# Infini-attention with a gated feed-forward on one core: another written-out order of the operations, the memory summed before it is masked, tanh in place, six probability buffers

## The chip, the cores and the metric

The kernel runs on one core of a Trainium2 chip. The metric is the device time of one execution in microseconds (us), the median of several runs. The core has TensorE (PE in the profile), VectorE (DVE), ScalarE (ACT), GpSimd (POOL) and SyncE (SP, which here only issues transfers). Each has its own queue of instructions and works through it in order: an instruction that waits holds all those behind it.

## The reference

```python
xn = layernorm(x)                       # x: 1 x 2048 x 448
q, k, v = xn @ wq, xn @ wk, xn @ wv     # 16 heads of 28, 4 segments of 512 rows
for s in range(4):                      # M = 0, z = 0 before the first segment
    p = softmax(causal(qs @ ks.T * 28**-0.5))      # inside the segment
    a_dot = p @ vs
    pq = phi(qs)                                   # phi(t) = t + 1 if t > 0 else exp(t)
    a_mem = (pq @ M) / (pq @ z + 1e-6)             # M, z from the earlier segments
    o = sigmoid(beta) * a_mem + (1 - sigmoid(beta)) * a_dot
    M = M + phi(ks).T @ vs;  z = z + sum(phi(ks))
s = concat(o) @ wo
f = (gelu(xn @ w_gate) * (xn @ w_up)) @ w_down     # inner width 1792
out = x + s * silu(f)
```

## The kernel before

A segment of 512 rows is four blocks of 128. Every piece of work is an operation with a name: the first digit after the letters is the segment, the next the block, step or chunk. Those that matter below:

- Start: `x00`, `x01`, `x02` load the blocks of the first segment (`x02` two of them, from ScalarE's queue; the other two from SP's), `warm_up` (L433) is eight matmuls on a zeroed tile, `bn`, `ag`, `xn`, `xc` are the layer norm (L489, L491, L514, L524), `trc` transposes (L457), `wv0`, `wk0`, `wq0` with a block's digit are projections (L575; seven matmuls to a block: the two half-width ones of two blocks are issued side by side as a "visit", `wr`). `nrm` with `rq` is part of a test of the logits' size: a column maximum and one small matmul.
- Attention of a segment: ten score steps `sc` (L846; sixteen 32-row matmuls with K = 32, into two pairs of PSUM banks), two exps to a step, `ex` (L861, ScalarE, 128 x 1024), causal masks `mk` on POOL (L872), products with the values `pv` (L908, sixteen matmuls a block). PSUM has four banks in two pairs, `pp0` and `pp1`, and four single ones, `ps0` to `ps3`. In segments 0 and 1 a score step may also write into `ps0` and `ps1`.
- Memory: `up` (L721) multiplies phi(k) with v of a finished segment; the matrix has all pairs of four heads, and `bdmask` keeps the blocks of a head with itself. `um` (L733), `ma` (L736) and `mc` (L739) make the masked bf16 memory `mbd` of it; `rd` (L759) reads it with phi(q). phi is an exp on ScalarE (`ex` of wq or wk, L687), a minimum on POOL (`mi`, L692), and `ph` on VectorE (L700 for q, L705 for k). The sums go out to DRAM and come back as reciprocals over the partitions (`den`, `dc`, `dg`, `rc`, `rd`, `rb`); `sm` (L770), `ca` (L814) and `cb` (L817) join both parts.
- Feed-forward: `gu` (gate and up, L964 for segment 0, L998 for the others), `ge` (gelu, L1005), `hm` (product, L1010, into `hT`), `dn` (down projection, L1055, fourteen matmuls a block), `th` and `sg` (L1064, L1067: tanh and a product; with it silu), `wo` (L1085), `fm`, `fa`, `st` (product, sum with x, store).

The feed-forward of a segment stands between the attention of two: gate and up of segment s, then the attention of segment s together with its down projections and the q, k, v of the next one. The table `TURNS` names all operations in one order. `arrange` (L157) walks it with assumed durations, gives every buffer the slot that comes free first, and returns the operations by the starts it has worked out; instructions are issued in this order, so it sets the order in all queues. Waits on the chip come from the data and buffers alone.

The lines of the memory, `s` being the segment that ended:

```python
um:  um[:] = u * bdmask                (VectorE, from PSUM)
ma:  macc[:] = macc[:] + um[:]         (POOL)
mc:  mbd[:] = macc[:]                  (POOL, cast to bf16)
```

Of the kernel before, what the change touches and what calls it, by code (L numbers as in the profile page):

```python
# [89 lines left out]
x00 x02 va0 warm qs1 va1 warm_up x01 wv vb1 ez0 qs2 ones wv2 kn0 qs4 nhalf wv3 wk vb0 kn1 bd wk2 ident wk3  # L90
bn00 ez1 xc_z su2 ag00 wq xc0 ep00 wq2 su3 trc00 xc2 bn01 bd0 evc00:ACT trc02 red_z qs0 wq3 xc3 evc02:ACT wv00
ag01 wgh xc1 sv2 trc03 qs3 wuh pw00 trc01 sv3 wv02 evc03:DVE evc01:DVE wv03 table wg0 xn00 ep03 wv01 ep01 wu0
ep02 pw02 wg4 wr0 pw03 wk00 evwv00:ACT du00 xn02 wu4 wk01 evwv02:ACT du02 xn03 x1 tr00 evwv03:DVE bd1 wk03
pw01 sq0 wg8 ev00:DVE wk02 sq1 xn01 du03 sq2 du01 wr1 evwv01:DVE wo0 wq03 evwk02:DVE evwk01:ACT wq01 sq3
evwk03:DVE evwk00:ACT tr01 rq2 tr02 tr03 sq4 ev01:DVE tk00 wq02 ev03:DVE exwk01 wq00 ev02:DVE rq1 exwk00 gh00
tk02 rq0 sq5 rq3 miwk00 gu00 evwq02:ACT wu8 rq5 evwq00:ACT miwk01 rq4 gu01 evwq01:ACT tq00 evwq03:DVE bn13
gu02 bn10 tq02 ge00 bn12 ge01 ag10 hm00 gu03 sq6 tq03 hm01 sq7 bn11 gh02 tk01 ag12 ag13 ag11 ep10 rq7 pw10
gu04 ge03 tq01 xn10 ge02 hm03 gu05 xn13 ge04 du10 du13 rq6 tr10 hm04 gu06 ge05 hm02 tr13 hm05 nrm gu07 nrm2
wo_in0 x2 xn11 gh06 xn12 x3 phwk00 wd_in0 gu08 ge07 tk03 du11 du12 hm07 gu09 ge08 tr11 ge06 hm08 gu010 hm06
ge09 wo_in3 tr12 bn20 gu011 hm09 bn21 wd_in1 bn23 beta gh010 bn30 ag30 gu012 ag20 ge011 bn22 ge010 bn33 hm011  # L100
gu013 ge012 hm010 hm012 sc00 ge013 ag21 ag23 ag22 wq10 ep20 hm013 pw20 wq11 bn31 wr1wq0 ex000 ag31 evwq10 ag33
ex001 bn32 tq10 sc01 wv10 xn20 ex010 xn22 xn21 gx mk000c0 ag32 evwq11 ex011 sc02 xn23 du20 dn000 ex020 mk011c0
tr20 phwk01 ex021 sc03 dn005 tr23 mk001c0 ex030 mk010c384 mk021c256 dn0010 mk020c0 ex031 tq11 bd2 mk011c384
wv11 mk010c0 th00 sc04 mk020c256 tr21 wr1wv0 sg00 mk021c0 ex040 bd3 evwv11 pv02 ex041 evwv10 tr22 mk040c0 sc05
mk031c0 ou000 wk10 ex050 ep30 mk040c384 wk11 wo_in1 pw30 ex051 sc06 mk041c0 wr1wk0 mk030c0 ex060 evwk10
mk041c384 wq12 mk050c0 evwk11 tk10 wq13 ex061 mk060c0 mk051c0 pv04 exwk10 mk061c384 tk11 wr1wq2 ou010
mk060c384 sc07 gates wk13 miwk10 evwq12 ex070 dn010 evwq13 tq12 mk061c0 ex071 xn30 gates2 sc08 dn015 ex080
den000 mk071c256 mk070c256 den010 xn31 dn0110 ex081 xn32 tq13 xn33 sc09 du30 phwk10 wk12 ex090 tr30 wr1wk2
th01 up0 mk081c0 evwk12 mk080c0 ex091 sg01 mk071c0 tk12 wv12 mk070c0 evwk13 exwq10 wv13 mk091c384 macc mk091c0
wr1wv2 tk13 mk090c384 exwq11 sc10 evwv13 mk090c0 pv07 miwq10 pv09 tr32 ou020 ex100 dn020 miwq11 ou030 ex101  # L110
evwv12 den020 wv20 phwq10 den030 wv21 tr33 sc11 wr2wv0 ex110 wv23 evwv21 dn025 dc00 evwv20 ex111 phwq11 tr31
dn0210 sc12 th02 mk100c0 wv22 dg00 ex120 rc00 mk111c384 wr2wv2 mc0 sg02 rd003 wq32 ex121 mk101c0 evwv23 wq33
rd000 mk110c0 evwv22 mk120c0 exwk11 rd11 rd002 mk121c0 sc13 ou111 mk110c384 wr3wq2 rd001 ex130 wq21 mk120c256
evwq33 xw10 mk111c0 rd10 evwq32 ex131 mk121c256 wq20 xw11 miwk11 ou101 rd12 den111 wr2wq0 ou121 sc14 rb000
wk20 evwq21 ex140 rb010 wk21 phwk11 wo_in2 ex141 wr2wk0 rb030 pv12 mk140c384 evwk21 mk141c384 sc15 evwq20
mk141c0 wq22 ex150 evwk20 tq20 wq23 cb00 ex151 dn030 tk20 mk140c0 wr2wq2 sc16 mk150c0 evwq23 dn035 mk131c0
# [40 lines left out]
def arrange(ops):  # L157
# [7 lines left out]
    for turn in order:  # L165
# [14 lines left out]
        if e == "POOL" or e == "DVE" and o.alone:  # L180
            s = max(s, port["DVE" if e == "POOL" else "POOL"])
# [5 lines left out]
        if e == "POOL" or e == "DVE" and o.alone:  # L187
            port[e] = s + occ
# [1423 lines left out]
```

## Time and profile before

| | us |
|---|---|
| median of three runs (229.08, 228.65, 228.87) | 228.87 |
| the profiled execution, whole | 230.46 |
| its span in the trace | 228.7 |
| around the span (230.46 - 228.7) | 1.76 |
| PE busy in the span | 218.6 |
| ACT, DVE, POOL busy | 158.5, 151.3, 125.9 |

The profiled execution took 1.59 us more than the median. Durations below are of that execution. A row of the timeline gives start, duration, engine, line, operation, output and inputs, the number of instructions in a row, and in brackets the idle time ahead of the first with what ended it. In rows by stretches every engine's busy time stands with its count, then the clock that TensorE was granted (1.00 is full), the share of the transfer engines and the rate of transfer. "Chain" rows are the chain of work that ended last, in order of time.

### The profile page before, as it was taken

How to read it: one execution, taken by the hardware profiler on the slowest of the kernel's cores; microseconds unless marked ns; L12 is line 12 of the kernel's file. 1: busy time of each engine (PE TensorE's matmuls, PEld its weight loads, DVE VectorE, ACT ScalarE, POOL GpSimd, SP SyncE). 2: the span in 40 equal slices, each digit the busy share in tenths (PEclk: the TensorE clock that was granted, in tenths of full speed). 3: DMA queues.
4: the chain of work that ended last, by engine and by line, in shares of the span. 5: the costliest groups of instructions: out<-in, count | busy, mean ns of one | idle time of the engine just before them, and what ended most of it. 6: DMA issues, size and time to landing. Idle time of an engine off the chain costs nothing.

```text
span 228.7 us, 4944 instructions
## 1 busy us (share of the span) xinstructions
PE 218.6 (96%) x1819; PEld 99.1 (43%) x1822; DVE 151.3 (66%) x285; ACT 158.5 (69%) x215; POOL 125.9 (55%) x223
## 2 busy tenths in 40 slices
PE   7999999899999999999999999999989999999990
PEld 3544343244443444444444344455533444445560
DVE  4699879936888867557756484677836457449152
ACT  4798335989978775999488779955777976335120
POOL 7422100569557598953076984270699975364620
PEclk9999999889999999999999999999999999999999
DMA  6899789493335799312655034125170111744012
GB/s 221 208 342 219 162 243 264 119 200 68 75 74 70 197 184 161 78 47 66 195 156 139 4 79 92 27 65 153 57 198 21 34 44 26 195 122 121 23 42 52
DMA packets 45606, 27.69 MB, mean 121 GB/s; under 512 B 30936, under 2 KB 40984, under 8 KB 45576
## 3 DMA queue, kind: packets, MB, share of 16 engines
q1 hardware_dynamic: 44600, 26.60, 49.6%
q10 hardware_dynamic: 976, 0.71, 1.0%
q8 instruction: 16, 0.26, 0.5%
q14 instruction: 14, 0.11, 0.2%
HBM read 17.38 MB, written 2.98 MB: 89 GB/s over the span
## 4 chain that ended last, share of the span: by engine, by line
PE 74%; DVE 15%; DMA 3%; issue 2%; POOL 2%; ACT 1%; ACTq 1%; SPq 1%; DVEq 0%; POOLq 0%
PE ps L1055 15%; PE ps L998 14%; PE pp L998 14%; PE ps L575 10%; PE pp L846 5%; PE ps L1085 5%; PE ps L908 4%; DVE hT L1010 3%; DVE st L489 2%; DMA x_sb<-in_A_x_dram 2%; DVE um L1151 2%; PE ps L721 1%; PE ps L759 1%; PE pp L1055 1%; PE ps L1121 1%
## 5 line engine op out<-in xcount | busy, mean ns | idle before, releaser
L861 ACT ACTIVATE pt<-pp 128x1024 bf16<-128x1024 f32 x76 | 73.9, 1028 | 16.3 <-PE pp L846 16.2
L872 POOL TENSOR_SCALAR_AFFINE_SELECT pt<-pt 128x256 bf16<-128x256 bf16 x128 | 50.5, 425 | 18.7 <-ACT pt L861 18.5
L1055 PE MATMUL ps<-wd_sb,hT 128*128 128x448 bf16 x196 | 43.0, 362 | 0.2 <-DVE e L611 0.2
L1005 ACT ACTIVATE gl<-pp 128x512 bf16<-128x512 f32 x29 | 17.0, 596 | 20.7 <-PE pp L998 12.2
L998 PEld LDWEIGHTS <-wg_sb 64*128 64x128 bf16 x252 | 22.8, 94 | 15.2 <-issue 2.5
L998 PEld LDWEIGHTS <-wu_sb 64*128 64x128 bf16 x252 | 23.1, 94 | 14.3 <-issue 0.4
L1055 PEld LDWEIGHTS <-hT 128*128 128x128 bf16 x210 | 19.5, 99 | 20.6 <-issue 5.3
L1005 ACT ACTIVATE gl<-ps 128x512 bf16<-128x512 f32 x27 | 15.6, 596 | 12.4 <-PE ps L998 9.7
L575 PEld LDWEIGHTS <-xnT 128*128 128x128 bf16 (+1 forms) x192 | 14.6, 97 | 20.4 <-issue 11.0
L1010 DVE TENSOR_TENSOR hT<-gl,ps 128x512 bf16<-128x512 bf16 x27 | 18.3, 682 | 7.6 <-ACT gl L1005 7.4
L817 POOL TENSOR_TENSOR oT<-oa,om 128x512 bf16<-128x512 f32 x12 | 15.7, 1317 | 12.4 <-DVE oa L814 12.4
L1010 DVE TENSOR_TENSOR hT<-gl,pp 128x512 bf16<-128x512 bf16 x29 | 19.1, 675 | 5.1 <-ACT gl L1005 5.1
L770 POOL TENSOR_TENSOR om<-om,rb 128x512 f32<-128x512 f32 x12 | 15.1, 1266 | 13.3 <-DMA rb<-rdr 11.8
L1076 POOL TENSOR_TENSOR oo<-sg,x_sb 128x448 bf16<-128x448 f32 (+1 forms) x14 | 14.6, 1049 | 12.2 <-DVE sg L1093 3.2
L692 POOL TENSOR_SCALAR e<-e 128x896 bf16<-128x896 bf16 (+1 forms) x12 | 11.8, 986 | 13.5 <-ACT e L687 13.4
L507 POOL TENSOR_TENSOR rs<-rs,nhalf 128x1 f32<-128x1 f32 (+1 forms) x7 | 5.3, 758 | 24.6 <-DVE rs L502 20.9
L998 PE MATMUL ps<-xnT,wu_sb 64*128 64x512 bf16 x63 | 17.0, 377 | 0.5 <-DVE hT L1010 0.5
L998 PE MATMUL ps<-xnT,wg_sb 64*128 64x512 bf16 x63 | 17.2, 377 | 0.0
L998 PE MATMUL pp<-xnT,wg_sb 64*128 64x512 bf16 x63 | 17.0, 376 | 0.0
L998 PE MATMUL pp<-xnT,wu_sb 64*128 64x512 bf16 x63 | 17.0, 376 | 0.0
L998 PE MATMUL pp<-xn,wg_sb 64*128 64x512 bf16 x63 | 17.0, 376 | 0.0
L998 PE MATMUL ps<-xn,wu_sb 64*128 64x512 bf16 x63 | 17.0, 376 | 0.0
(137 smaller groups left out, 425.9 us busy)
## 6 DMA issues: line engine op xcount, KB each, us to landing
rb<-rdr SPq DMA_DIRECT2D x28, 256.0 KB
out_dram<-oo SPq DMA_DIRECT2D x15, 112.0 KB
wd_sb<-in_B_w_down_dram SPq DMA_DIRECT2D x2, 784.0 KB
x_sb<-in_A_x_dram SPq DMA_DIRECT2D x3, 448.0 KB
xn<-xnT SPq DMA_DIRECT2D x6, 192.0 KB
rdr<-dc SPq DMA_DIRECT2D x28, 32.0 KB
wg_sb<-in_B_w_gate_dram SPq DMA_DIRECT2D x2, 384.0 KB
wu_sb<-in_B_w_up_dram SPq DMA_DIRECT2D x2, 384.0 KB
```

Source lines behind the costliest of these rows:

```text
L575: nc.tensor.matmul(out=self.bank.ap()[:, 0:D], lhsT=self.xT.ap()[r, c, n * P:(n + 1) * P], rhs=self.w[r, c, :], **kw)
L692: o = gps(f"mi{nm}{s}{half}", n / 1024, lambda: nc.gpsimd.tensor_scalar(out=t(), in0=t(), scalar1=1.0, scalar2=0.0, op0=ALU.min, op1=ALU.max),
L770: oU[s, g, 1] = t, gps(f"sm{s}{g}", 1.22, lambda t=t, r=r: nc.gpsimd.tensor_tensor(out=t.ap(), in0=t.ap(), in1=r.ap(), op=ALU.mult), deps= ...
L817: oT[s][1].append(gps(f"cb{s}{g}", 1.22, lambda g=g, t=t, tm=tm: nc.gpsimd.tensor_tensor(out=dst.ap()[:, g, :], in0=t.ap(), in1=tm.ap(), o ...
L846: nc.tensor.matmul(out=S2[i // 2].ap(i % 2)[:, c0:c0 + n], lhsT=kT[s][0].ap()[r, g, kb * P:(kb + 1) * P], rhs=qT[s][0].ap()[r, g, kb * P:L ...
L861: nc.scalar.activation(out=dst, in_=src, func=ACT.Exp, scale=scale)
L872: nc.gpsimd.affine_select(out=v, in_=v, pattern=[[0, 2], [1, P]], compare_op=ALU.is_ge, fill=0.0, base=0, channel_multiplier=-1)
L998: nc.tensor.matmul(out=bf[fc].ap(i), lhsT=w, rhs=x, start=c == 0, stop=c == 2 * NC3)
L1005: a = act(f"ge{s}{fc}", L, lambda: nc.scalar.activation(out=gl.ap(), in_=bf[fc].ap(0), func=ACT.Gelu_apprx_tanh), func="gelu", deps=[o], a ...
L1010: nc.vector.tensor_tensor(out=hT[s][0].ap()[:, fc, :], in0=gl.ap(), in1=bf[fc].ap(1), op=ALU.mult), deps=[a] + held,
L1055: nc.tensor.matmul(out=bank.ap()[:, 0:D], lhsT=hT[s][0].ap()[:, fc, b * P:(b + 1) * P], rhs=wd_sb[:, fc, :], start=(fc == 0), stop=(fc == ...
L1076: o = op(f"fa{s}{b}{h}", eng, lambda: (nc.vector if o.on == "DVE" else nc.gpsimd).tensor_tensor(out=oo.ap()[:, r], in0=t.ap()[:, r], in1=x ...
```

## The change

1. `TURNS` is another table; it reorders all five queues.
2. `arrange` returns the operations in the table's own order, and its rule for VectorE and POOL working at once, and some assumed durations, are others. That has an effect through order and slots only.
3. Memory: `macc` is added up unmasked, on VectorE straight from PSUM; the mask is applied in the cast on POOL. The tile `um` and two `ma` are gone.
4. `th` writes into the tile of `sg`, and the pool of two tanh tiles is gone.
5. Six buffers for the probabilities in place of five.
6. Loads and the first load of ScalarE's table no longer stand in a fixed sequence; the first exps of segment 0 no longer have to stand behind its last gelu.

```diff
 TURNS = """
-x00 x02 va0 warm qs1 va1 warm_up x01 wv vb1 ez0 qs2 ones wv2 kn0 qs4 nhalf wv3 wk vb0 kn1 bd wk2 ident wk3
-bn00 ez1 xc_z su2 ag00 wq xc0 ep00 wq2 su3 trc00 xc2 bn01 bd0 evc00:ACT trc02 red_z qs0 wq3 xc3 evc02:ACT wv00
+va0 qs0 kn1 vb0 nhalf warm warm_up x01 kn0 x00 x02 wv3 wv table wv2 qs2 xc_z bn01 su2 bn00 ag00 ez1 ident x1
+wk2 wk wk3 wq2 wuh wq wu0 va1 wgh bd bd0 qs4 qs1 vb1 qs3 xc0 trc00 su3 ep00 ag01 xc1 xc2 xc3 trc01 ep01 pw00
...
-    return sorted(ops, key=lambda o: o.start)
+    return [named[turn.partition(":")[0]] for turn in order]
...
-        um = const.tile([P, G, P], F32, name="um")
+        red_t = const.tile([P, P], F32, name="red")
...
-        pt_p = slots(5, [P, HG, L], BF16, "pt")
+        pt_p = slots(6, [P, HG, L], BF16, "pt")
...
-        th_p = slots(2, [P, D], F32, "th")
...
         def load(eng, name, dst, src, kb, rate=320.0):
-            o = op(name, {eng: (0.5, 2.0)}, ..., after=first[-1:], prio=-1000, kb=kb, rate=rate)
+            o = op(name, {eng: (0.5, 1.5)}, ..., prio=-1000, kb=kb, rate=rate)
...
         table_op = op("table", ..., func=ACT.Exp),
-            deps=[nhalf_in], after=wv_in, prio=-400)
+            deps=[nhalf_in], prio=-400)
...
             if s == 0:
-                o = dve("macc", ..., lambda: nc.vector.tensor_tensor(
-                    out=macc[:], in0=uv(), in1=bd, op=ALU.mult), deps=[o] + bd_in, ...)
+                o = dve("macc", ..., lambda: nc.vector.tensor_copy(out=macc[:], in_=uv()), deps=[o], ...)
             else:
                 o = dve(f"um{s}", ..., lambda: nc.vector.tensor_tensor(
-                    out=um[:], in0=uv(), in1=bd, op=ALU.mult), deps=[o, mem["acc"], ok_op], ...)
-                o = gps(f"ma{s}", 1.22, lambda: nc.gpsimd.tensor_tensor(
-                    out=macc[:], in0=macc[:], in1=um[:], op=ALU.add), deps=[o], prio=pr)
-            mem["acc"] = o
-            mem["cast"] = gps(f"mc{s}", 0.58, lambda: nc.gpsimd.tensor_copy(out=mbd[:], in_=macc[:]), ...)
+                    out=macc[:], in0=macc[:], in1=uv(), op=ALU.add), deps=[o, mem["cast"]], ...)
+            mem["cast"] = gps(f"mc{s}", 1.22, lambda: nc.gpsimd.tensor_tensor(
+                out=mbd[:], in0=macc[:], in1=bd, op=ALU.mult), deps=[o] + bd_in, ...)
...
-                            after=[first] if exps else [first, att.get("gelu_end")],
+                            after=[first, att.get("gelu_end") if s and not exps else None],
...
             a = act(f"th{s}{b}", D, lambda: nc.scalar.activation(
-                out=th.ap(), in_=bank.ap()[:, 0:D], func=ACT.Tanh, scale=0.5), ...)
+                out=t.ap(), in_=bank.ap()[:, 0:D], func=ACT.Tanh, scale=0.5), ...)
             ... vector.scalar_tensor_tensor(
-                out=t.ap(), in0=th.ap(), scalar=1.0, in1=bank.ap()[:, 0:D], ...)
+                out=t.ap(), in0=t.ap(), scalar=1.0, in1=bank.ap()[:, 0:D], ...)
```

A few lines of the changed kernel have other numbers: L491 is L493, L542 is L544, L611 is L613, L692 is L694, L700 is L702, L705 is L707, L721 is L723, and the cast of the memory is L738.

The first place is VectorE at the start of segment 0's attention. `hT` is the product of the feed-forward, `st`, `mv`, `rs` and `xn` belong to the layer norms of segments 2 and 3, `qs`, `kn`, `e` and `vaug` receive the projections of segment 1 out of PSUM, and L705 is phi(k) of segment 0. Before:

```order
L1010 TENSOR_TENSOR hT_85<-gl0_127,ps3_95 128x512
L489 BN_STATS st0_138<-x_sb3_66 128x6
L491 BN_AGGR mv0_142<-st0_138 128x2
L611 CAST qs_107<-ps1_93 128x16x28
L491 BN_AGGR mv0_142<-st3_141 128x2
L489 BN_STATS st2_140<-x_sb3_66 128x6
L514 TENSOR_SCALAR xn0_96<-x_sb2_65,mv1_143,rs0_144 128x448 x3
L491 BN_AGGR mv0_142<-st2_140 128x2
L611 CAST e1_106<-ps2_94 128x16x28
L514 TENSOR_SCALAR xn0_96<-x_sb2_65,mv1_143,rs0_144 128x448
L542 COPY xn0_96<-xn0_96 128x4x64
L705 SCALAR_TENSOR_TENSOR kn0_86<-kn0_86,e0_105 128x32x28
```

After, at the same place:

```order
L1010 TENSOR_TENSOR hT_85<-gl2_130,ps2_94 128x512
L493 BN_AGGR mv1_142<-st0_137 128x2
L707 SCALAR_TENSOR_TENSOR kn0_86<-kn0_86,e0_105 128x32x28
L613 CAST qs_107<-ps3_95 128x16x28
L1151 TENSOR_REDUCE red_83<-pt1_109 64x16
L613 CAST kn1_87<-ps2_94 128x16x28
L445 TENSOR_SCALAR igate_79<-igate_79 128x2
L613 CAST e0_105<-ps0_92 128x16x28
L613 CAST kn1_87<-ps1_93 128x16x28
L613 CAST vaug1_89<-ps2_94 128x16x28
L613 CAST vaug1_89<-ps3_95 128x16x28
L707 SCALAR_TENSOR_TENSOR kn0_86<-kn0_86,e1_106 128x32x28
```

The layer norm of segment 2 has moved ahead, into the feed-forward, that of segment 3 behind; six evictions stand together, and a phi(k), a reduction and a gate (L445) stand ahead of some of them. On PE, step `sc01` writes `pp0` and `pp1` now, where before it wrote `ps0`, `ps1` and `pp0`.

The second place is VectorE in the gate and up of segment 1. L700 is phi(q) of segment 2 (`pqT`), the L1010 rows are `hm`, which read the banks that later `gu` steps write. Before:

```order
L705 SCALAR_TENSOR_TENSOR kn0_86<-kn0_86,e1_106 128x32x28
L744 COPY oa3_116<-ps2_94 128x512
L744 COPY oa2_115<-ps3_95 128x512
L1010 TENSOR_TENSOR hT_85<-gl2_129,pp1_91 128x512
L1010 TENSOR_TENSOR hT_85<-gl0_127,pp0_90 128x512
L700 SCALAR_TENSOR_TENSOR pqT0_104<-qT0_100,e1_106 128x1024
L1010 TENSOR_TENSOR hT_85<-gl1_128,ps1_93 128x512
L1010 TENSOR_TENSOR hT_85<-gl2_129,ps3_95 128x512
```

After:

```order
L707 SCALAR_TENSOR_TENSOR kn0_86<-kn0_86,e1_106 128x32x28
L1010 TENSOR_TENSOR hT_85<-gl2_130,pp1_91 128x512
L744 COPY oa3_117<-ps3_95 128x512
L744 COPY oa2_116<-ps2_94 128x512
L1010 TENSOR_TENSOR hT_85<-gl0_128,ps1_93 128x512
L1010 TENSOR_TENSOR hT_85<-gl1_129,pp0_90 128x512
L1010 TENSOR_TENSOR hT_85<-gl0_128,ps3_95 128x512
L702 SCALAR_TENSOR_TENSOR pqT0_104<-qT0_100,e1_106 128x1024
```

phi(q) has moved behind two more products.

The third place is POOL around the second memory update, at the change from segment 2's feed-forward to segment 3's attention. Before:

```order
L770 TENSOR_TENSOR om3_120<-om3_120,rb3_124 128x512
L1076 TENSOR_TENSOR oo0_136<-sg1_133,x_sb1_64 128x448
L817 TENSOR_TENSOR oT0_126<-oa0_113,om3_120 128x512
L736 TENSOR_TENSOR macc_81<-macc_81,um_83 128x512
L739 CAST mbd_82<-macc_81 128x512
L817 TENSOR_TENSOR oT0_126<-oa2_115,om1_118 128x512
L872 AFFINE_SELECT pt3_111<-pt3_111 128x2x128 x2
```

After:

```order
L770 TENSOR_TENSOR om2_120<-om2_120,rb3_125 128x512
L770 TENSOR_TENSOR om0_118<-om0_118,rb0_122 128x512
L1076 TENSOR_TENSOR oo1_136<-sg3_134,x_sb1_64 128x448
L738 TENSOR_TENSOR mbd_82<-macc_81,bdmask_80 128x512
L1076 TENSOR_TENSOR oo0_135<-sg1_132,x_sb1_64 128x448
L770 TENSOR_TENSOR om1_119<-om1_119,rb2_124 128x512
L817 TENSOR_TENSOR oT0_127<-oa0_114,om1_119 128x512
L872 AFFINE_SELECT pt4_112<-pt4_112 128x2x128
```

One row writes the memory `mbd` where two did, and it stands inside the feed-forward of segment 2. On PE the matmuls of that update (`up2`) stand behind step `sc26` of segment 2's attention, before behind `sc30`.

More of the change, by code (lines that the diff above doesn't have):

```diff
@@ L100 @@
[L100 to L104, printed above, removed]
@@ L187, in arrange @@
         if e == "POOL" or e == "DVE" and o.alone:
-            port[e] = s + occ
+            other = port["DVE" if e == "POOL" else "POOL"]
+            if other[0] <= s < other[1]:
+                s = other[1]
+            port[e] = s, s + occ
         if o.kb is not None:
@@ L350, in load @@
         def load(eng, name, dst, src, kb, rate=320.0):
-            o = op(name, {eng: (0.5, 2.0)}, lambda: (nc.sync if eng == "SP" else nc.scalar).dma_start(
-                out=dst, in_=src), after=first[-1:], prio=-1000, kb=kb, rate=rate)
+            o = op(name, {eng: (0.5, 1.5)}, lambda: (nc.sync if eng == "SP" else nc.scalar).dma_start(
+                out=dst, in_=src), prio=-1000, kb=kb, rate=rate)
             first.append(o)
@@ L1043, in down @@
         def down(s, b, pr):
[L1044 removed]
+            bank, t = Buf(B_, END if s == LAST else ONE), Buf(sg_p)
             o = None
```

168 lines of the change are left out of this document (86 added, 82 removed).

## The prediction

> **What bounds the kernel now.** I read the busy times first, then the chain of work that ended last, then stretches, then the waits of TensorE.
>
> ```profile
> PE 218.6 (96%) x1819; PEld 99.1 (43%) x1822; DVE 151.3 (66%) x285; ACT 158.5 (69%) x215; POOL 125.9 (55%) x223
> ...
> PE 74%; DVE 15%; DMA 3%; issue 2%; POOL 2%; ACT 1%; ACTq 1%; SPq 1%; DVEq 0%; POOLq 0%
> ```
>
> TensorE is busy for 96% of the span and carries 74% of the chain. The change leaves its matmuls as they are, so it can gain only where TensorE stands idle or runs slowly, and it loses where it makes new such places. The stretches say where these are:
>
> ```profile
> core 0: us, PE busy (x) PEld busy (x) DVE busy (x) ACT busy (x) POOL busy (x), PEclk, DMA share, GB/s
> 6.10:38.60 32.50, 32.23 (x185) 14.06 (x189) 28.54 (x75) 19.99 (x38) 6.19 (x8) 1.00 1.01 237
> 38.60:50.70 12.10, 10.88 (x79) 4.03 (x79) 8.28 (x23) 10.98 (x15) 5.86 (x13) 0.86 0.79 176
> 103.80:106.00 2.20, 1.65 (x17) 0.69 (x15) 2.17 (x6) 2.17 (x3) 0.50 (x1) 1.00 0.39 119
> 167.00:169.00 2.00, 1.12 (x7) 0.41 (x5) 0.30 (x1) 1.67 (x3) 1.94 (x4) 1.00 0.84 227
> ...
> 223.10:228.70 5.60, 0.18 (x5) 0.03 (x1) 1.25 (x4) 0.25 (x1) 0.32 (x1) 0.97 0.21 53
> ```
>
> ```profile
> PE ps L759 <- POOL mbd L739: 0.9, 1, 0.9
> PE ps L846 <- DVE qs L611: 0.7, 1, 0.7
> PE ps L998 <- DVE hT L1010: 0.5, 1, 0.5
> ```
>
> The worst is 38.6 to 50.7, the start of segment 0's attention, with 1.2 us idle and a clock of 0.86. Small holes stand at 104 and 168. The last 5.6 us after TensorE's last matmuls (a silu, products, sums and a store) have the same steps after the change, and I cost them at nothing. Inside the worst stretch:
>
> ```profile
> 40.60:44.00 3.40, 2.28 (x22) 0.84 (x21) 3.37 (x11) 3.40 (x5) 0.86 (x2) 1.00 0.35 83
> 44.00:47.50 3.50, 3.50 (x13) 1.16 (x12) 1.56 (x3) 3.21 (x6) 3.14 (x7) 0.51 0.78 177
> ...
> 38.56:59.44 20.88, 19.62 (x153) 7.71 (x153) 14.94 (x37) 19.76 (x28) 13.17 (x29) 0.92 0.60 134
> ```
>
> TensorE is busy for 67% (2.28 of 3.40) of one stretch, and in the next, about as long, it runs at half the clock. Over the 20.88 us between the steps sc00 and sc09 the clock of 0.92 means 0.08 x 20.88 = 1.67 us lost, and ScalarE is busy for 19.76 of the 20.88: it is the true bound there.
>
> **The change part by part.** *Segment 0's attention.* Full rates, from the chain in order of time:
>
> ```profile
> 54.47 0.66 PE ps L908 x16
> 55.13 0.29 PE ps L575 x2
> ...
> 55.75 0.67 PE ps L575 x3
> 56.42 0.95 PE ps L1055 x5
> 59.51 0.33 PE pp L846 x8
> ```
>
> That is 0.66 us for a value product, 0.145 for a half-width matmul, 0.19 for a matmul of 448 columns, 0.33 for a score step. Before, sc00 to sc09 holds 9 steps (2.97), 27 projection matmuls (5.13), 8 half-width ones (1.16), 28 of the down projection (5.32) and two value products (1.32): 15.9 us in 20.88, so 5.0 lost, 1.67 of it by the clock. After, the order puts about 19.1 us of the same kind there (three more projections, five blocks' worth of half-width matmuls, dn020, up0): work that was later is drawn into the holes. What holds ScalarE:
>
> ```profile
> 38.95 1.28 ACT L861 ACT_TABLE_LOAD   x1
> 40.24 1.94 ACT L861 ACTIVATE pt<-pp 128x1024 bf16<-128x1024 f32 x2
> 46.35 1.94 ACT L861 ACTIVATE pt<-pp 128x1024 bf16<-128x1024 f32 x2 [0.29 <-PE pp L846]
> 48.74 0.54 ACT L1064 ACTIVATE th<-ps 128x448 f32<-128x448 f32 x1 [0.45 <-PE ps L1055]
> 55.12 1.01 ACT L687 ACTIVATE e<-kn 128x896 bf16<-128x896 bf16 x1
> ```
>
> The table is loaded 1.67 us after sc00 starts; 18 exps at 0.97 are 17.5, one exp of phi 1.0, one tanh 0.54: 20.7 us at least. So the loss is at least 20.7 - 19.1 = 1.6, and at most 3.4 could be gained. VectorE's queue there:
>
> ```profile
> 44.31 1.29 DVE L705 SCALAR_TENSOR_TENSOR kn<-kn,e 128x896 bf16<-128x896 bf16 x1
> ```
>
> Before, sc01 waits 0.7 for a cast (the second row of the list of waits), which stands behind layer norms. After, these are gone, but the phi(k) of 1.29 in this row stands ahead of the casts. So I take a loss of 2.2 to 2.4 rather than 1.6, a gain of 2.6 against the profiled execution. Against the median I take less. This execution is 1.59 us above the median, almost the 1.67 that the half clock costs, which would fit if the timed runs did not have it. Without it the loss before is 3.3, and the gain 1.0. I take -1.0, with ends -3.4 and +3.0 (below).
>
> *Feed-forward of segment 1, step gu18.*
>
> ```profile
> 101.73 1.04 POOL L692 TENSOR_SCALAR e<-e 128x1024 bf16<-128x1024 bf16 x1
> 102.81 1.23 DVE L700 SCALAR_TENSOR_TENSOR pqT<-qT,e 128x1024 bf16<-128x1024 bf16 x1 [2.45 <-POOL e L692]
> 103.76 0.38 PE L998 MATMUL ps<-xnT,wg_sb 64*128 64x512 bf16 x1
> 104.69 0.37 PE L998 MATMUL ps<-xnT,wu_sb 64*128 64x512 bf16 x1 [0.55 <-DVE hT L1010]
> ```
>
> phi(q) stands idle for 2.45 us at the head of VectorE's queue, waiting for POOL; the product behind it is late, and its bank with it. The two matmuls of a pair lie side by side, so rows follow each other at about half of 0.38; from 103.76 to 104.69 TensorE loses 0.7. After, two more products stand ahead of phi(q), and that bank is free in time: -0.7, ends -0.7 and 0. What is late next is the product behind hm16, whose bank is wanted several steps later.
>
> *The second memory update.*
>
> ```profile
> 166.96 1.26 POOL L736 TENSOR_TENSOR macc<-macc,um 128x512 f32<-128x512 f32 x1
> 168.29 0.61 POOL L739 CAST mbd<-macc 128x512 bf16<-128x512 f32 x1
> ...
> 166.19 1.88 PE L1055 MATMUL ps<-wd_sb,hT 128*128 128x448 bf16 x9
> ...
> 171.71 2.98 POOL L872 TENSOR_SCALAR_AFFINE_SELECT pt<-pt 128x256 bf16<-128x256 bf16 x8 [0.51 <-ACT pt L861]
> ```
>
> TensorE's first read of the memory waits for the cast (0.9 in the list of waits). Nine matmuls at 0.19 from 166.19 end at 167.9, the read starts 0.9 after the modelled end of 168.07, so 1.05 us are lost. After, the update stands a whole feed-forward earlier, and its one POOL instruction inside that feed-forward: -1.05. POOL's price of an update falls from 1.26 + 0.61 = 1.87 to one tensor operation, which I take at 1.26 (bf16 out of f32, two inputs; ends 0.61 and 1.87). On VectorE the sum has the same shape as the masked product, no change. But POOL's sums of both parts now move into segment 3's attention: eight tensor operations (10.1) and twelve masks at 0.37 (4.5) are 14.6 us behind sc30 before pv32 can start, which TensorE reaches after about 15 us of its own work. I add +0.4, ends 0 and +1.4. Together -0.65.
>
> *Start.*
>
> ```profile
> 1.26 3.60 PE L433 MATMUL ps<-oT 128*128 128x512 bf16 x8 [1.26 <-DVE oT L386]
> 4.65 0.63 PE L457 MATMUL ps<-oT,hT 128*128 128x128 bf16 x4
> 6.09 0.93 PE L575 MATMUL ps<-wv_sb,xnT 128*128 128x448 bf16 x3
> ...
> 2.79 0.63 DVE L489 BATCH_NORM_STATS2 st<-x_sb 128x6 f32<-128x448 bf16 x1 [1.59 <-DMA x_sb<-in_A_x_dram]
> ```
>
> Block 0 is loaded first on SP's queue before, and its statistics start at 2.79. After, the layer norm of block 0 needs the second transfer of that queue, and all four groups of transposes stand ahead of the first projection. One transfer later I put at about 0.9 us for the transposes and 0.8 for the projections, of which later order takes back a part: +0.5, ends 0 and +1.0. The logit test's matmul leaves the stretch 6.1 to 38.6, which has 0.27 us idle: -0.25, ends -0.27 and 0.
>
> *Around the last values.*
>
> ```profile
> 210.24 4.01 POOL L817 TENSOR_TENSOR oT<-oa,om 128x512 bf16<-128x512 f32 x3 [0.72 <-DVE oa L814]
> ...
> 215.87 0.92 PE L1085 MATMUL ps<-wo_sb,oT 128*128 128x448 bf16 x4
> ```
>
> POOL is done at 214.25, wo at 215.87 reads the result: 1.6 us in hand. After, the last two value products (pv37, pv39) stand behind steps gu32 and gu33, some 3 us later, and the rest of that chain with them. 3 - 1.6 = +1.4 is the upper end, 0 the lower; I take +0.3, since down projections can run meanwhile.
>
> *Small ones.* TensorE's changes between tile shapes fall by two of 132; three projection matmuls at 0.19 are 0.57, and take 0.67 in the row at 55.75 behind a score step, so a change costs 0.1: -0.2, ends -0.2 and 0. Tanh in place, and a sixth probability buffer, I cost at nothing: no row shows ScalarE or TensorE waiting for such a tile. ScalarE's table load ahead of the other work at the start lies beside warm_up.
>
> Sum against the median: -1.0 - 0.7 - 0.65 + 0.5 - 0.25 + 0.3 - 0.2 = -2.0, so 228.87 - 2.0 = 226.9 us. Against the profiled execution it would be -3.6.
>
> **The rivals.** *The half clock was in the timed runs too, and goes.* Then segment 0 gives 2.6 in place of 1.0: 226.9 - 1.6 = 225.3. For it: the busy share of 67% precedes the half clock directly, nothing says that a timed run has another share. Against it: the 1.59.
>
> *The full clock comes later at the start.* Row:
>
> ```profile
> 3.10:6.50 3.40, 3.20 (x15) 1.31 (x13) 2.68 (x9) 3.34 (x7) 1.63 (x10) 1.00 1.08 326
> ```
>
> The warm-up's matmuls take 0.45 us each (3.60 for 8), the next projections 0.19, so the full rate comes between 6 and 8 us. This stretch is 94% busy. With the transposes 0.9 us later it would be 68%, as low as the 67% that went ahead of the half clock in segment 0. Another 3.4 us at half rate cost 1.7: 228.6. [...]
>
> *Segment 0 in lock-step.* This ends on the slower side. sc01 goes to pp0 and pp1 after the change, whose exps must be done first. If order and banks make each step wait for the exps and each pair of exps for its step, nine rounds cost 9 x (1.94 + 0.29) = 20.1, with 1.67, 1.0 and 0.54 on ScalarE 23.3 us for 19.1 of work. That loses 4.2 where the median's 3.3 stood, and a TensorE busy for 82% on the whole has thinner parts early, so one or more stretches at half clock, 1.67 each. With one and some 0.4 of VectorE's phi(k), segment 0 costs +3.0: 226.9 + 1.0 + 3.0 = 230.9. The rest of the sum is -1.0, so it decides from +1.0 there. Against it: much independent work (projections, dn000) stands between the steps.
>
> *POOL holds pv32 or wo.* Both upper ends (1.4 - 0.4 and 1.4 - 0.3) would give 226.9 + 2.1 = 229.0, one of them 228.
>
> **How the numbers follow.** A measurement here tells 0.2% (0.46 us) from no change. The sum, 226.9 (own range 226.0 to 227.9): 0.42. Half clock gone from timed runs, 225.3: 0.20. Later clock at the start, 228.6: 0.12, of it 0.04 faster, 0.06 the same, 0.02 slower. Lock-step, 230.9: 0.12. POOL, 228 to 229: 0.14, of it 0.09 faster, 0.04 the same, 0.01 slower. So faster 0.75, same 0.10, slower 0.15. The range reaches from 225.0, just below the second case, to 229.2, above the late clock and POOL, and leaves out the lock-step and little else.
>
> **What would show it.** Segment 0: sc00 to sc09 still near 20.9 us or less, with the same clock or better and more matmuls; lock-step would show idle TensorE on exps and 23 us. gu18 without its wait on L1010; the first read of memory in segment 3 without one on `mbd`. At the start, the first projection near 6.9 in place of 6.09, and 0.19 us a matmul from there, or 0.38 if the clock is late. A wait of pv32 or wo on POOL shows the last rival. The prediction is wrong if new holes, which no row of before can show, come in the feed-forwards, where TensorE is now without any.

## The result and the profile after

The changed kernel takes 236.22 us (median of four runs, 235.77 to 236.76) where the kernel before takes 228.98 in the same comparison: a ratio of 1.032, interval 1.029 to 1.036. It is 7.2 us slower. The profiled execution took 235.77 us, its span is 234.0.

The head of the page after, busy times and chain:

```profile
PE 219.1 (94%) x1822; PEld 98.6 (42%) x1822; DVE 156.3 (67%) x285; ACT 159.4 (68%) x215; POOL 128.3 (55%) x220
...
PE 53%; DVE 20%; POOL 7%; SPq 6%; DMA 5%; issue 4%; ACT 3%; ACTq 0%; DVEq 0%; POOLq 0%
```

TensorE's busy time is nearly the same (219.1 for 218.6), but its share of the chain has fallen from 74% to 53%: VectorE, POOL, SP's queue and transfers now take turns at holding it. The list of TensorE's waits after, in us, times and the longest:

```profile
PE ps L1055 <- DVE vaug L613: 2.0, 1, 2.0
PE pp L577 <- DMA wv_sb<-in_A_wv_dram: 1.9, 1, 1.9
PE ps L435 <- DVE oT L388: 1.3, 1, 1.3
PE ps L759 <- DVE pqT L702: 1.1, 1, 1.1
PE ps L908 <- POOL pt L872: 0.9, 1, 0.9
PE pp L846 <- DMA qT<-e: 0.8, 1, 0.8
PE ps L459 <- DVE rs L504: 0.7, 1, 0.7
```

The waits of before (the memory's cast, sc01 for a VectorE cast, gu18 for a product) are gone, all three. Others stand in their place, at the start and in the attention of segments 1 and 3. The start, TensorE's timeline:

```profile
1.26 3.59 PE L435 MATMUL ps<-oT 128*128 128x512 bf16 x8 [1.26 <-DVE oT L388]
5.51 1.99 PE L459 MATMUL ps<-oT,hT 128*128 128x128 bf16 x16 [0.66 <-DVE rs L504]
9.42 2.40 PE L577 MATMUL pp<-wv_sb,xnT 128*128 128x448 bf16 x6 [1.93 <-DMA wv_sb<-in_A_wv_dram]
11.62 2.08 PE L577 MATMUL ps<-wv_sb,xnT 128*128 128x448 bf16 x6
...
14.34 0.73 PE L577 MATMUL ps<-wk_sb,xnT 128*128 128x448 bf16 x3
```

The first projection begins at 9.42 in place of 6.09, since wv is not there: its main part lands at 9.38, before at 5.52 (the time at which its semaphore is full). And its twelve matmuls take 4.2 us, not the 2.3 that they take at 0.19: TensorE was idle for 1.9 us, and its rate is half until about 13. That is read from the matmuls alone; the clock in the row of this stretch is 1.00, as it is in the prediction's row over the warm-up at 0.45 us a matmul. In sp_order below, where the six matmuls take the same 2.40, the clock reads 0.50 (7.92 to 11.33). The row here:

```profile
9.40:13.60 4.20, 4.18 (x12) 1.57 (x11) 2.37 (x9) 0.00 (x0) 0.00 (x0) 1.00 0.91 254
```

TensorE works without a pause from 9.42 (4.18 us busy of the 4.20), and the full rate is there some 4 us later (three projection matmuls in 0.73 at 14.34); what brings it no row shows. With wv in time (wv_main_first below) the rate is full from the first projection on (six matmuls in 1.33). That the wait for wv brings the half rate doesn't follow: two other kernels waited 1.5 and 1.8 us for it and ran at the full rate (see the part on why the prediction was wrong).

To see where the rest went I took, for each stage, the time between two named steps less TensorE's work between them at its full rate (448 columns in 0.19 us). That is the time lost, in us, each entry rounded by itself; the two columns on the right are kernels of the experiments:

| stage | before | after | wv_first_phq3 | old_to_gu14 |
|---|---|---|---|---|
| start to sc00 | 5.5 | 9.9 | 5.8 | 5.0 |
| sc00 to sc10 (segment 0's attention) | 7.2 | 5.4 | 5.2 | 5.9 |
| sc10 to gu10 (segment 1's attention) | 3.8 | 5.8 | 5.8 | 4.2 |
| gu10 to sc20 | 1.6 | 0.7 | 0.7 | 0.7 |
| sc20 to gu20 | 3.2 | 3.5 | 3.4 | 3.3 |
| gu20 to sc30 | 0.9 | 0.7 | 0.9 | 1.1 |
| sc30 to gu30 (segment 3's attention) | 4.5 | 6.2 | 3.3 | 3.3 |
| gu30 to the last matmul | 0.8 | 0.9 | 0.9 | 0.9 |
| sum | 27.5 | 33.1 | 26.2 | 24.6 |

The sum rises by 5.6 from before to after, the span by 5.3. (The profiled execution of before lies 1.5 above its median and that of after 0.5 below, so the time differs by 7.2.)

### The profile page after: what moved, and what is told of

It reads as the page before. It is cut to its first block, busy times and chain, and to the rows that moved or that the text cites. A ratio compares the mean times of both kernels' runs of the same rounds, so it can differ in the third digit from the quotient of the medians.

```text
span 234.0 us, 4919 instructions
## 1 busy us (share of the span) xinstructions
PE 219.1 (94%) x1822; PEld 98.6 (42%) x1822; DVE 156.3 (67%) x285; ACT 159.4 (68%) x215; POOL 128.3 (55%) x220
## 4 chain that ended last, share of the span: by engine, by line
PE 53%; DVE 20%; POOL 7%; SPq 6%; DMA 5%; issue 4%; ACT 3%; ACTq 0%; DVEq 0%; POOLq 0%
PE ps L998 15%; PE pp L998 13%; PE ps L577 6%; PE ps L1055 6%; PE ps L1085 4%; DMA wv_sb<-in_A_wv_dram 3%; DVE hT L1010 3%; DVE pqT L702 3%; PE ps L908 3%; POOL oT L817 3%; SPq L626 3%; PE pp L846 2%; POOL pt L872 2%; SPq L548 2%; DVE oa L814 2%
## 5 line engine op out<-in xcount | busy, mean ns | idle before, releaser
L872 POOL TENSOR_SCALAR_AFFINE_SELECT pt<-pt 128x256 bf16<-128x256 bf16 x128 | 52.2, 445 | 20.2 <-ACT pt L861 20.1
L1055 PE MATMUL ps<-wd_sb,hT 128*128 128x448 bf16 x210 | 44.1, 353 | 2.0 <-DVE vaug L613 2.0
L1010 DVE TENSOR_TENSOR hT<-gl,ps 128x512 bf16<-128x512 bf16 x28 | 18.8, 682 | 21.2 <-ACT gl L1005 21.2
L1005 ACT ACTIVATE gl<-ps 128x512 bf16<-128x512 f32 x28 | 16.5, 595 | 16.6 <-PE ps L998 14.1
L770 POOL TENSOR_TENSOR om<-om,rb 128x512 f32<-128x512 f32 x12 | 16.0, 1349 | 21.0 <-DMA rb<-rdr 21.0
L1005 ACT ACTIVATE gl<-pp 128x512 bf16<-128x512 f32 x28 | 16.1, 596 | 14.7 <-PE pp L998 8.1
L577 PEld LDWEIGHTS <-xnT 128*128 128x128 bf16 (+1 forms) x192 | 15.4, 99 | 24.1 <-issue 15.1
L1010 DVE TENSOR_TENSOR hT<-gl,pp 128x512 bf16<-128x512 bf16 x28 | 18.4, 677 | 2.3 <-ACT gl L1005 2.3
L694 POOL TENSOR_SCALAR e<-e 128x896 bf16<-128x896 bf16 (+1 forms) x12 | 11.9, 995 | 11.7 <-ACT e L689 11.7
L998 PE MATMUL ps<-xnT,wu_sb 64*128 64x512 bf16 x66 | 17.8, 377 | 0.0
L846 PE MATMUL pp<-qT,kT 32*128 32x512 bf16 (+3 forms) x244 | 16.9, 302 | 1.0 <-DMA qT<-e 0.8
L998 PE MATMUL ps<-xn,wg_sb 64*128 64x512 bf16 x66 | 17.8, 376 | 0.0
L1076 POOL TENSOR_TENSOR oo<-sg,x_sb 128x448 bf16<-128x448 f32 x13 | 14.4, 1105 | 5.3 <-DVE sg L1093 3.4
```

The costliest lines, as they stand in the source:

```text
L577: nc.tensor.matmul(out=self.bank.ap()[:, 0:D], lhsT=self.xT.ap()[r, c, n * P:(n + 1) * P], rhs=self.w[r, c, :], **kw)
L694: o = gps(f"mi{nm}{s}{half}", n / 1024, lambda: nc.gpsimd.tensor_scalar(out=t(), in0=t(), scalar1=1.0, scalar2=0.0, op0=ALU.min, op1=ALU.max),
L770: oU[s, g, 1] = t, gps(f"sm{s}{g}", 1.22, lambda t=t, r=r: nc.gpsimd.tensor_tensor(out=t.ap(), in0=t.ap(), in1=r.ap(), op=ALU.mult), deps= ...
L846: nc.tensor.matmul(out=S2[i // 2].ap(i % 2)[:, c0:c0 + n], lhsT=kT[s][0].ap()[r, g, kb * P:(kb + 1) * P], rhs=qT[s][0].ap()[r, g, kb * P:L ...
L872: nc.gpsimd.affine_select(out=v, in_=v, pattern=[[0, 2], [1, P]], compare_op=ALU.is_ge, fill=0.0, base=0, channel_multiplier=-1)
L998: nc.tensor.matmul(out=bf[fc].ap(i), lhsT=w, rhs=x, start=c == 0, stop=c == 2 * NC3)
```

## The experiments

All are built from the changed kernel's code and differ in the table only, so each diff shows the words of the table that move. Line numbers in their profiles are one lower than in the changed kernel. A ratio is to the kernel before in the same comparison, where its median was 228.8 to 229.3.

**All edits but the table.** The table holds the operations in the order in which the kernel before issued them.

> All edits of the change but the table: masked cast on POOL, unmasked sum, tanh in place, six probability buffers, with the operations in the order in which the kernel before issued them. Theory (the new order carries the whole loss): 229.0, within 0.5 of the kernel before. Rival (the new memory update or the tanh in place makes waits of its own): 231 or more, with waits on the masked cast or on the tile of tanh.

Measured: 229.06 us, ratio 1.000 (0.998 to 1.003). The masked cast, tanh in place and six buffers cost nothing and bring nothing that can be measured (the interval reaches 0.6 us to either side); the loss is in the order. The list of waits shows what the memory's edit does by itself:

```profile
PE ps L758 <- POOL mbd L737: 0.3, 1, 0.3
```

The first read of the memory waits 0.3 where it waited 0.9; 0.6 us is about what this comparison can't tell from nothing. The half clock in segment 0's attention is not there in this profile: 6.0 us lost in that stage against 7.2 before, with a mean granted clock of 0.996 for 0.992. This profiled execution took 230.09 us all the same, 1.0 above its median, so an execution can lie that far above the median without a half clock.

**Segment 1's x, two ways.** I suspected the 448 KB of segment 1's x, third on SP's queue after the change.

```diff
-... wv2 qs2 xc_z ... x1 wk2 wk wk3 ...        (x1_late_new_order: the new order)
+... wu4 wg4 x1 ...                            (and bn1, ag1, xn1, tr1, x2, x3 later)
```

> The changed kernel, with the load of segment 1's x (448 KB) moved from the third place of SP's queue to behind the gate and up weights, and the layer norm and transposes of segment 1 that need it moved into the gate and up of segment 0. Theory (this transfer holds up the weights): the first projection starts before 7 us in place of 9.42, step sc00 at 38.5 to 39.3 in place of 42.64, time 232 to 232.6. Rival (the start is lost to the order of the other loads, the early table load and the transposes): sc00 stays above 41 and the time above 235.

Measured: 243.6 us, ratio 1.063 (1.055 to 1.072), a miss. The later x2 held VectorE's queue through segment 2's layer norm and TensorE for 6 us at gu09, and 6.8 us at a clock of 0.50 followed (39.76 to 46.58); the start itself improved little (first projection at 8.36, wv's main part at 8.32 with x1 out of its way). So x1 isn't by itself what makes wv late.

```diff
-... wv3 wk wk2 ...                            (x1_early_old_order: the old order)
+... wv3 x1 wk wk2 ...
```

> The order of the kernel before, with one load moved: segment 1's x third in SP's queue, ahead of wk. Theory (this transfer alone costs the start): 232 to 233, the first projection at 8.5 to 9.5. Rival (it is the other parts of the new start): 229 to 229.5.

Measured: 229.76 us, ratio 1.003 (1.002 to 1.005): the rival's value nearly. wv's main part landed at 5.14. My theory that x1 alone costs the start fell.

**The old head with the new rest.**

> The changed kernel with all operations up to the first gate and up step in the order before, and everything behind in the new order (segment 1's layer norm goes into gate and up of segment 0). Theory (start and late stalls add up): 231.5 to 232.3, sc00 at 38.6, the stalls in segments 0, 1 and 3 as in the changed kernel. Rival (the late stalls come of the late start and go with it): 229 or less.

Measured: 239.2 us, ratio 1.043 (1.037 to 1.049). The first projection is in time (6.12), but the same seam at gu09 costs a wait of 5.9 us as two runs above, and 6.8 us at a clock of 0.50 again (37.26 to 44.09), so sc00 comes later still (47.7). It tells nothing of the sum. The waits in segment 3 are there (2.0 and 0.9 us); that they stay with an early sc00 only the next run shows.

**Two loads swapped.** In x1_early_old_order wv's main part is the first of its weight on ScalarE's queue, in both kernels with a late start a half-width part of 56 KB is. So:

```diff
-... x00 x02 wv3 wv table wv2 ...
+... x00 x02 wv wv3 table wv2 ...
```

> The changed kernel with two loads of ScalarE's queue swapped: the main part of wv (128 partitions, 336 KB) ahead of its first half-width part (64 partitions, 56 KB), as before the change; nothing else. Theory (the half-width part ahead of it holds the main part up): it lands near 5.5 in place of 9.38, sc00 comes 2.5 to 4 us earlier, 232 to 233.7. Rival (x1 and the other half-width loads on SP's queue hold it up as well): it lands at 7 to 8.5, the time falls by 1 us at most, or by nothing.

Measured: 231.75 us, ratio 1.007 (1.003 to 1.011), so 4.5 us of the 7.2 come back with two words swapped. TensorE's timeline of that run:

```profile
5.37 1.98 PE L458 MATMUL ps<-oT,hT 128*128 128x128 bf16 x16 [0.51 <-DVE rs L503]
7.15 1.33 PE L576 MATMUL pp<-wv_sb,xnT 128*128 128x448 bf16 x6
8.32 1.30 PE L576 MATMUL ps<-wv_sb,xnT 128*128 128x448 bf16 x6
```

wv's main part lands at 5.05, nothing waits for it (a half-width part costs 0.2 at 9.77), and six projection matmuls take 1.3 us where they took 2.4 and 2.1. The transposes are as late as in the changed kernel (5.4), and the rate is full all the same. sc00 starts at 38.8 in place of 42.6, and the waits in segment 3 stay, 1.7 and 0.9. The reverse, in the old order:

```diff
-... wv wv2 wv3 wk ...
+... wv3 wv wv2 wk ...
```

> The order of the kernel before, with one load moved: the first half-width part of wv (56 KB) ahead of the main part on ScalarE's queue; x1 stays where it was. Theory (the place in the queue alone, with the loads of SP's queue that then come ahead of it, makes wv late): the main part lands at 8 to 9.4 in place of 5.5, the first projection starts at 8 or later, 231.5 to 233. Rival (only together with segment 1's x ahead of it): it lands before 6.5, 229 to 229.6.

Measured: 233.6 us, ratio 1.020 (1.014 to 1.027), with runs at 230.1, 233.3, 233.9 and 235.2. The profiled one is the fastest of them and has the wait:

```profile
PE ps L576 <- DMA wv_sb<-in_A_wv_dram: 1.8, 1, 1.8
```

wv's main part lands at 7.81. The swap alone makes wv late and the kernel slower. How much it costs here is uncertain: the profiled run lost 1.0, with the projections at the full rate (three matmuls in 0.73), the others 4 to 6, and no trace shows theirs. Nor is it clear what x1 ahead of wv adds: in the four kernels with the changed kernel's loads wv's main part lands at 8.26 to 9.38, in this one and with x1 late at 7.81 and 8.32. ScalarE's issues are 0.5 us apart, so the swap costs 0.57 us in issue (1.89 for 1.32) and 2 to 4 us in landing. In the changed kernel and here a large load of SP's queue (x1, the main part of wk) is then issued ahead of wv's main part; that this is what delays it is argued only. With all loads in the order before:

> The changed kernel with its 21 first loads issued in the order before, except that segment 1's x stays third on SP's queue; the table load and all other work stay in the new order. Theory (the order of the loads makes the loss at the start, x1 being harmless by the run with x1 alone): first projection at 6.1 to 6.9, sc00 at 38.9 to 39.5, 232 to 232.7. Rival (the new order of the layer norm, transposes and evictions loses it): sc00 above 41, above 234.5.

Measured: 231.54 us, ratio 1.009 (1.006 to 1.013), the same as with two loads swapped. wv's main part lands at 6.33; the first projection is later than expected (7.29), as the transposes wait 1.1 for VectorE. sc00 starts at 38.7. The rest of the new load order, with x1 third and the early table load, costs nothing beside it that shows.

**Segment 3's phi(q).** Before, VectorE did both of them in segment 2's feed-forward:

```profile
153.76 2.35 DVE L700 SCALAR_TENSOR_TENSOR pqT<-qT,e 128x1024 bf16<-128x1024 bf16 x2
```

After, VectorE's timeline in segment 3's attention, then POOL's and TensorE's:

```profile
168.41 1.43 DVE L702 SCALAR_TENSOR_TENSOR pqT<-qT,e 128x1024 bf16<-128x1024 bf16 x1
169.77 1.64 DVE L814 TENSOR_TENSOR oa<-oa,rb 128x512 f32<-128x512 f32 x1
171.33 2.05 DVE L702 SCALAR_TENSOR_TENSOR pqT<-qT,e 128x1024 bf16<-128x1024 bf16 x1
173.31 4.02 DVE L814 TENSOR_TENSOR oa<-oa,rb 128x512 f32<-128x512 f32 x3
177.25 0.61 DVE L613 CAST vaug<-ps 128x448 bf16<-128x448 f32 x1
```

```profile
168.72 2.13 POOL L738 TENSOR_TENSOR mbd<-macc,bdmask 128x512 bf16<-128x512 f32 x1
170.82 1.48 POOL L1076 TENSOR_TENSOR oo<-sg,x_sb 128x448 bf16<-128x448 f32 x1
172.26 2.24 POOL L770 TENSOR_TENSOR om<-om,rb 128x512 f32<-128x512 f32 x1
```

```profile
177.91 1.10 PE L1055 MATMUL ps<-wd_sb,hT 128*128 128x448 bf16 x5 [2.02 <-DVE vaug L613]
```

9 us of VectorE's work stand ahead of a cast that TensorE needs for its next bank. The second phi(q) takes 2.05 us and POOL's masked cast 2.13; where they do not overlap with such work they take 1.22 (below) and 1.15 (at 76.00 in this profile). VectorE and POOL slow one another in these rows. By the ends of the rows (start plus duration) they even take turns: POOL's cast ends at 170.85, VectorE's join at 171.41, POOL's sum at 172.30, the second phi(q) at 173.38, POOL's join at 174.50. Each ends 0.56 to 1.12 us behind the one before it, a little less than it takes alone (0.68, 1.03, 1.22, 1.26). Alone the two phi(q) and four joins of VectorE would take 2 x 1.22 + 4 x 0.68 = 5.2 us by estimate in place of the 9. The phi(q) and the joins have two inputs in SBUF. VectorE's products of the feed-forward just before (hT<-gl,ps and hT<-gl,pp, one input in PSUM) are not slowed in the same profile: the three at 163.35, 165.78 and 167.28 take 0.68 to 0.69 us each beside POOL's joins, and those take 1.27 for one (163.04) and 2.49 for two (165.28). Why the one pair slows and the other does not, no row shows.

```diff
-... fm12 phwq30 rb230 rb210 ca23 phwq31 dn220 ...
+... ge28 ge26 hm26 hm28 phwq30 ... hm210 phwq31 ...
```

> The changed kernel with the two phi(q) of segment 3 (L702) moved on VectorE's queue from segment 3's attention back into the gate and up of segment 2. Theory (these, the joins L814 and POOL's two-input operations slow one another there and the cast of v stands behind them): the wait of 2.0 on that cast and part of the 0.9 on POOL's masks go, 234.0 to 234.8. Rival (the joins alone hold the cast up): the wait stays above 1.3, 235.6 to 236.4.

Measured: 235.25 us, ratio 1.026 (1.020 to 1.032). The waits on the cast and on the masks went, and 2.9 us were won in segment 3's attention; but 2.7 were lost ahead of it. VectorE there:

```profile
160.01 1.22 DVE L701 SCALAR_TENSOR_TENSOR pqT<-qT,e 128x1024 bf16<-128x1024 bf16 x1
161.34 0.69 DVE L1009 TENSOR_TENSOR hT<-gl,ps 128x512 bf16<-128x512 bf16 x1
163.74 2.28 DVE L701 SCALAR_TENSOR_TENSOR pqT<-qT,e 128x1024 bf16<-128x1024 bf16 x1 [1.71 <-POOL e L693]
```

The second phi(q) waits for a minimum on POOL, which stands behind a join that waits for a transfer, and the products behind it are late: sc30 waits 1.5 and 0.8 for them. With that minimum moved too:

```diff
-... gu26 sm22 miwq31 ...
+... miwq30 miwq31 ... gu26 sm22 ...
```

> The changed kernel with both phi(q) of segment 3 back in segment 2's gate and up and their second minimum ahead of the joins, the loads as in the changed kernel. Theory (two separate losses, the loads 4 to 5 us and this 2.5): 233.3 to 234.2. Rival (with the late start this stage is not on the path): 235.5 or more.

Measured: 232.42 us, ratio 1.018 (1.013 to 1.023): 3.8 us back, more than either range allowed. By the profiles 0.7 of it lies ahead of sc00, where nothing was changed (41.9 for 42.6). And with the loads swapped as well:

> The changed kernel with wv's main part first on ScalarE's queue, both phi(q) of segment 3 back in segment 2's gate and up, and their second minimum on POOL (L694) ahead of the joins (L770) that wait for a transfer. Theory (the two are separate losses; the hold-up that the phi(q) met when it was moved back alone was that minimum behind a join): no wait over 0.6 at the change from segment 2 to 3 nor on the cast of v or the masks there, 228.8 to 229.6. Rival (a new wait in the gate and up again): 230.5 or more.

Measured: 229.19 us, ratio 1.001 (0.997 to 1.005). Two loads swapped and three instructions moved take back 7.0 of the 7.2 us. By the table the 2.0 lost in segment 1's attention stay, and the new order's gains elsewhere make up for them. The parts, 4.5 and 3.8, add up to more, 8.3: 0.7 of the 3.8 was the start's, and single runs of these kernels scatter by 3 to 4 us.

**SP's queue in segment 0 and 1.**

```diff
-... tq13 ... tk13 ... tq12 ... tr32 ... den030 den020 ... tr33 dc00 ...
+... tq13 tq12 ... tk13 ... den030 den020 tr32 ... dc00 tr33 ...
```

> The changed kernel with four transfers moved on SP's queue in segment 0's attention: the transpose of q of segment 1's block 2 directly behind that of block 3, and the sums of the first segment's heads (to DRAM and back) ahead of two transposes of segment 3's rows. Theory (these two transfers behind transposes that take 1.2 us each make the waits of sc10 for q, 0.8, and of the first read of the memory, 1.1): both waits go, 234.2 to 235.0. Rival (VectorE's queue is late anyway, and another wait takes their place): 235.7 to 236.5.

Measured: 234.9 us, ratio 1.020 (1.011 to 1.029). The waits on q and on the memory's first read went, and in the list of waits stands

```profile
PE ps L576 <- DMA xnT<-xn: 2.0, 1, 2.0
```

for a transpose of the rows of segment 3, which had been moved back. From sc00 to gu10 as much is lost as without the change (11.2 us); what the time fell by lies ahead of sc00, in an earlier landing of wv (first projection at 8.30 for 9.42). So the time fell into the theory's range without its reason. The rival had it right that another wait takes their place; its reason, a late VectorE, the run doesn't show. It shows that a transfer put forward on SP's queue made another late.

**Versions meant to beat both.**

> As the last one, but with all operations ahead of the first gate and up step in the order before (segment 1's x third on SP's queue, as the new order behind needs it early). Theory (the new order is better than the old in the feed-forward of segment 1 and in segment 0's attention, and worse at the start and in segment 3 alone): 227.5 to 228.6, faster than before. Rival (the loss between sc10 and gu10 eats it up): 228.9 to 230.

Measured: 233.4 us, ratio 1.018 (1.012 to 1.024), outside both ranges. A new seam: gu02 waits 2.5 us for an eviction that stands behind segment 1's layer norm on VectorE, and 3.4 us at half the clock follow (the run's mean granted clock is 0.987). One transfer moved on top of it:

> As the last one, with one more transfer moved on SP's queue: the transpose of q of segment 1's block 2 directly behind that of block 3. Theory (sc10's wait for q is on the path): 0.5 to 1.2 below the last one. Rival (the queue is full, what is moved back is late in its place): the same within 0.3.

Measured: 232.7 us, ratio 1.014 (1.008 to 1.020), the difference too small to tell by these runs. The last seam is at a place where both orders have done nearly the same work, eleven operations apart:

> The order of the kernel before up to step gu14 of segment 1's feed-forward, the new order behind it, with segment 3's phi(q) back in segment 2's gate and up. Theory (lost TensorE time by stage adds up: the old order loses about 17 us up to there, the new one 9.3 behind it, 26.3 in place of 27.4 before): 227.8 to 228.6, faster than before. Rival (the seam or the placing of phi(q) makes a new wait, as at the seam after the start): 229.5 or more.

Measured: 227.79 us (227.54 to 227.89), ratio 0.995 (0.993 to 0.997): faster than both kernels. TensorE's longest waits there:

```profile
PE ps L434 <- DVE oT L387: 1.3, 1, 1.3
PE ps L576 <- DVE sg L1066: 0.7, 2, 0.5
PE ps L845 <- DVE qs L612: 0.5, 1, 0.5
```

The first is the start; no other wait above 0.5 is left. The gain is small but real: the slowest run here is faster than the fastest of the kernel before (228.35). By the table it lies mostly in segment 1's feed-forward (0.9) and segment 3's attention (1.2). The 1.3 in segment 0's attention is no more than the half clock costs in before's profile (1.7), and segment 2 gives nothing.

## Why the prediction was wrong

I forecast 226.9 (225.0 to 229.2), and it was 236.2. Point by point:

- *Start* (+0.5, ends 0 and +1.0): the step that failed most. Measured: +4.4 us lost. I priced the order of x's two first blocks and put ScalarE's table load "beside warm_up". The head of the table shows, in the lines quoted with the change, `x02 wv3 wv table wv2` for `wv ... wv2 ... wv3`; I read past it, and priced neither the weight that the first projection waits for nor what is issued ahead of it. The swap of these two loads takes 4.5 us back, which shows it.
- *The full clock later at the start* (rival, 228.6): the half rate came, until about 13 us, and cost about 1.9 us (twelve matmuls in 4.2 for 2.3). The rival's 3.4 us at half rate were an estimate, the length of the half-clock stretch in segment 0 of before (3.50 us at 0.51 in its row) carried over to the start; here the half rate lasted from 9.42 to about 13. Late transposes alone don't bring it: they are as late with wv in time (5.37 for 5.51), and the rate is full (six matmuls in 1.33). The wait for wv alone doesn't either. Of six kernels that waited for it, four (0.7, 1.5, 1.9 and 2.3 us) took 2.4 us for the next six matmuls; the two others (1.5 in x1_late_new_order, 1.8 in wv3_first_old_order) ran them at the full rate. None that didn't wait had the half rate for more than three of them. What decides is open.
- *The second memory update* (-0.65): the gain came (the wait of 0.9 is gone), but segment 3's attention lost 1.7 in all. I counted POOL's queue ahead of pv32 (+0.4; its wait was 0.9, so a part of the last rival came) and not VectorE's, where the two phi(q) had come in, ahead of the cast that TensorE waits 2.0 for. They appear in the sum nowhere, and moving them back won 2.9 us in this stage. My price of the masked cast, 1.26, is 1.15 alone and 2.13 beside them.
- *Segment 1's attention* was left out. The table moved its transposes on SP's queue, and 2.0 us were lost from sc10 to gu10. Which part of the new order loses them is open: with the old order up to gu14 the stage loses 4.2 as against 5.8, but sp_order took its two longest waits away without gaining there.
- *Segment 0's attention* (-1.0 on the median's basis): right in kind. From sc00 to sc10 5.4 are lost after, 6.0 in the old order without the half clock, 7.2 with it: -0.6 and -1.8. That the half clock was missing from the timed runs is not shown. For it: parts_old_order has the same time as before and no half clock in its profile. Against my reading of the 1.59 us: that profile lies 1.0 above its own median without one. The lock-step didn't come.
- *gu18* (-0.7): right, -0.9 for that stage. *Around the last values* (+0.3): +0.1. Tanh in place and the sixth buffer: nothing, as said.

With the start and segment 3 as measured (+4.4 for +0.5, +1.7 for -0.65) and segment 1's +2.0 the sum of -2.0 becomes +6.3, near the 7.2. In the feed-forwards, where I would have looked for new holes, none came.

## What to carry to other kernels

When an order is replaced, go through every queue at its head first, loads above all: for each transfer that the first matmul needs, name what is issued ahead of it before and after, on all queues together. A new order that fills holes can move work beside that of another engine which slows it: here the second phi(q) took 2.05 us beside POOL's sum and join for 1.22 alone. So count VectorE and POOL together where a profile shows such a pair. And an order from elsewhere is not good or bad as a whole: lost TensorE time by stage tells where to cut, and the cut belongs where both orders have done nearly the same work (the seams elsewhere made new waits of 2.5 to 6 us here).

## What was not expected of the hardware

A load of 56 KB ahead of one of 336 KB on the same queue, 0.57 us of issue, moved the landing of the larger by 2 to 4 us: it lands at 5.05 to 6.33 in the ten profiles in which it is first on ScalarE's queue, and at 7.81 to 9.38 in the six in which it is second. Why so much is open. In five of the six a large load of SP's queue was issued 0.15 to 0.17 us ahead of it, but in x1_late_new_order only one of 56 KB was, and it landed at 8.32 all the same.

How busy TensorE is doesn't settle the clock by itself in these runs. In phq3_only and sp_order it was busy for 1.32 and 1.57 us of the 3.4 ahead of 8.59 and 7.92, and the clock was 0.50 for the next 3.4; in wv3_first_old_order and x1_late_new_order it was busy for 1.65 and 1.85 of the 3.4 ahead of 9.50 and 9.03, and the clock stayed at 1.00. In segment 0 of before, 2.28 of 3.40 went ahead of a half clock (0.51 from 44.00 to 47.50). So the 67% that the prediction took for a sign of the half clock is no bound.

Single runs scatter by 3 to 5 us in some kernels (229.6 to 233.6 with wv's main part first in the new order, 230.1 to 235.2 with it second in the old), by 1.0 in the changed kernel and by 0.4 in the last one. Why is open too.
